# Down stage of a fused attention and gated-MLP block: the first outer Strassen product gets a second Strassen level

## The chip, the cores and the metric

The kernel runs on one core of one Trainium2 chip. The metric is the device time of one execution in microseconds; the matrix unit is TensorE (PE in the profile), the elementwise engines are VectorE (DVE), ScalarE (ACT) and GpSimd (POOL), and SyncE (SP) issues most of the DMA transfers. Each engine works through its own queue of instructions in order, and engines wait for one another by semaphores.

## The reference

The computation is one transformer block on 2048 tokens of width 1024 in bf16: a layer norm, linear attention with 32 heads, a residual, a second layer norm, a gated MLP of width 3584, and a residual.

```python
x = A_x
h = x + attention(layernorm(x), A_wqkv, A_wo)
n = layernorm(h)
gate, up = n @ B_W_gate, n @ B_W_up          # [2048, 1024] @ [1024, 3584]
hidden = (gate * (gate > 0)) * up
h2 = h + hidden @ B_W_down                   # [2048, 3584] @ [3584, 1024]
```

The change is in the last line's product, the down stage, and at its border with the gate/up stage before it.

## The kernel before

Most products are computed by Winograd's form of Strassen's algorithm: left and right operands are cut in two by two blocks, four sums of left blocks (s1 to s4) and four of right blocks (t1 to t4) are formed, and seven block products (m1 to m7) take the place of eight. With left blocks a11, a12, a21, a22 and right blocks b11 to b22:

- s1 = a21 + a22, s2 = s1 - a11, s3 = a11 - a21, s4 = a12 - s2
- t1 = b12 - b11, t2 = b22 - t1, t3 = b22 - b12, t4 = b21 - t2
- m1 = a11 b11, m2 = a12 b21, m3 = s4 b22, m4 = a22 t4, m5 = s1 t1, m6 = s2 t2, m7 = s3 t3

The partial sums of the products are formed in PSUM: m1, then m6, then m7, then m4 are accumulated in one and the same PSUM tile (tag A), and a copy or an add takes the running sum out after each of them. m2 has a tile of its own. m5 and then m3 accumulate in another one.

**Gate/up stage.** The hidden width is handled in 14 pairs of chunks of 128. One call of `quad` (L902) does the seven products for one chunk and one set of 512 tokens; a call is one window of the schedule, six products of eight 128x512 matmuls, while m4 and m3 of the previous window run inside it. ScalarE copies running sums (L921) and applies the ReLU (L926, L933). VectorE adds (L925), multiplies gate and up (L929, L936) and forms the sums of hidden blocks that the down stage will read (L751 to L759). These sums are stored to DRAM (L754, L761). The tiles of the block h11, which the first outer product reads, stay in SBUF as `x1`. In the first window of each later group of four, a further product over part of the contraction is itself done by Strassen (`cross`, L988); its operand sums and results live in tiles of a small pool: `cs` (left sums), `ct` (weight sums), and `cr` (results, read by `g0` of later windows). Each window has six slots (`slot`, L1071) in which pending VectorE work is put between the named steps. In the last two windows no such work is left.

**Down stage.** The outer level cuts tokens (two halves of 1024), hidden width (two halves of 14 chunks) and output columns (two halves of 512) and makes seven outer products, in the order 1, 2, 6, 5, 3, 7, 4 (`OUTER`, L1025). I call them op0 to op6. The left sums come from DRAM (`x_dram`), the weight sums too (`t_dram`).

- For the outer products in `INNER` (L1026) a second Strassen level is used (`inner`, L1387): seven products of 28 matmuls of 128x256, with 4 token tiles times 7 chunks. Its operand sums are formed by VectorE from a queue (`queue_sums`, L1306; `pop` takes the next one), and results leave by `snap` (L1415) and `sink` (L1422).
- op0 (outer product 1) and op5 (outer product 7) are plain (`plain_mm`, L1233): four pairs of token tiles times two contraction halves, each a block of 14 matmuls of 128x512.
- op0's result is copied by ScalarE to the fp32 tiles `u2` (`sink1`, L1470), four copies. Later products add to `u2` and `u5`.
- Outputs are put into the four-deep tile `o` by VectorE and stored by an accumulating DMA from GpSimd, or for the last product by a plain one (`put`, L1366). The residual h is loaded in `load_h` (L1359).

**Order.** TensorE, VectorE and ScalarE run in the order in which the program text issues their work from the start of the gate/up stage, and SP from the opening of `dpool` (L1266). Around the border the text is: m7 of the last window, op0's first plain block, then the last window's `g3`, `x3`, m4, `rg`, `x2`, m3, `g1`, `x1`. Then the gate/up pools are closed and `dpool` takes their memory. Then come the loads for op1 (L1463 to L1467), the other seven blocks of op0, and the loop over op1 to op6 (L1494). Within that loop a second-level product takes m4 and m3 of the second-level product before it in between its own m2 and m6.

Of the kernel before, what the change touches and what calls it, by code (L numbers as in the profile page):

```python
# [8 lines left out]
ALU = mybir.AluOpType  # L9
FP32 = mybir.dt.float32  # L10
# [72 lines left out]
def block_kernel(ctx: ExitStack, tc: tile.TileContext, x, wqkv, wo, wg, wu, wd, out, H: int):  # L83
# [195 lines left out]
    with ExitStack() as actx:  # L279
# [668 lines left out]
    KQ = KH // 2  # L948
    cross_s = [ipool.tile([P, KQ, SW], FP16, tag=f"cs{k}", name=f"cs{k}") for k in range(3)]
    cross_a = [[hnT[s][0][:, KH + j * KQ:KH + (j + 1) * KQ, :] for j in range(2)] for s in range(NS)]  # L950

    def cross_left_sums():

        (a11, a12), (a21, a22) = cross_a
        s1, s2, s4 = (v[:] for v in cross_s)
        tt = nc.vector.tensor_tensor
        return [
            lambda: tt(out=s1, in0=a21, in1=a22, op=ALU.add),
            lambda: tt(out=s2, in0=s1, in1=a11, op=ALU.subtract),
            lambda: tt(out=s4, in0=a12, in1=s2, op=ALU.subtract),  # L960
            lambda: tt(out=a21.bitcast(FP16), in0=a11, in1=a21, op=ALU.subtract),
        ]

    def cross_left(m):
        (a11, a12), (a21, a22) = cross_a
        s1, s2, s4 = (v[:] for v in cross_s)
# [120 lines left out]
    for r, (wt, f, fi, toks) in enumerate(runs):  # L1087
# [3 lines left out]
        for n, s in enumerate(toks):  # L1091
# [14 lines left out]
            if k:  # L1106
                want = -(-len(fill) // max(nwin - 2 - k, 1))
                for p in range(want):
                    work.insert(len(work) if held_back else min(len(work), 2 * p + 1), fill.pop(0))
            held_back = []  # L1110
            if k == NE and not snaps:
                base = [new_snap() for i in range(4)]
                res = {(0, 0): base[0], (1, 0): base[0]}
                for q in ((0, 1), (1, 1)):
                    res[q] = ipool.tile([P, 2, SW], FP32, tag=f"cr{q[0]}", name="cr")
                snaps.extend((base[1], base[3], base[2]))
                snaps.insert(0, snaps.pop())
# [123 lines left out]
    for i in range(NS):  # L1241
        for kh in range(2):
            xtiles[0, i, kh] = x1[i][kh][:]
    fview = []
    for n in range(2):
        t = fpool.tile([P, 4 * D], BF16, tag="wraw", bufs=2, name="xd")
        fview.append(t[:, 0:FQ * SW].rearrange("p (f t) -> p f t", f=FQ))
    ftile = fpool.tile([P, FQ * SW], BF16, tag="wt", name="xd")
    xs_free = [ftile[:, 0:FQ * SW].rearrange("p (f t) -> p f t", f=FQ).bitcast(FP16)]
    for i, t in ((1, fview[0]), (0, fview[1])):  # L1250
        xtiles[1, i, 0] = t
        load_x(1, i, 0)
    first_ps = [acc("A")]
    plain_mm(first_ps[0], 0, 0, 0)
    prv["g3"]()
    prv["x3"]()
    prv["m4"]()
    prv["rg"]()
    prv["x2"]()
    prv["m3"]()  # L1260
    prv["g1"]()
    prv["x1"]()
    sctx.close()
    mctx.close()

    dpool = ctx.enter_context(tc.tile_pool(name="dpool", **reuse))  # L1266
    ctx.enter_context(tc.manual_schedule(engines={ET.SP}))

    for x in range(2):
        wtiles[2 + x] = dpool.tile([P, FQ, DW], BF16, tag=f"w{x}", name="w")[:]  # L1270
        xtiles[1, 1 - x, 1] = dpool.tile([P, FQ, SW], BF16, tag=f"x{x}", name="x")[:]
    for x in range(3):
        xs_free.append(dpool.tile([P, FQ, SW], FP16, tag=f"xs{x}", name="xs")[:])
    held_s = {}
    free_s = list(range(4))

# [29 lines left out]
    def queue_sums(op):  # L1306
# [42 lines left out]

        queue.extend((op, f.__name__, f) for f in (t1, s1, s2, t2, s4, s3, t3, t4))  # L1350

    def new_u(nm):
        return [dpool.tile([P, NT, DW], FP32, tag=nm, bufs=2, name=nm) for s in range(NS)]

    u2, u5 = new_u("u2"), new_u("u5")
    out_v = of.rearrange("(t p) d -> p t d", p=P)
    hres = {}

    def load_h(k, s):  # L1359

        if k == OUTER[-1]:
            v = dpool.tile([P, NT, DW], BF16, tag="h", bufs=2, name="h")
            nc.scalar.dma_start(out=v[:], in_=h_dram[s][:])
            hres[k, s] = v

    def put(k, s, ts, cs, ps, m, with_h=True, eng=nc.scalar):  # L1366

        i, j = outs[k]
        o = dpool.tile([P, NT * HW], BF16, tag="o", bufs=4, name="o")
        ov = o[:, 0:(ts.stop - ts.start) * (cs.stop - cs.start)].rearrange("p (t d) -> p t d", t=ts.stop - ts.start)  # L1370
# [12 lines left out]

    base_of = {2: u2, 6: u2, 5: u2, 3: u5, 4: u2}
    u_of = {6: u2, 5: u5}

    def inner(op):  # L1387

        k, st, base = op["k"], {}, base_of[op["k"]]
        tag = "XY"[op["n"] % 2]  # L1390

# [29 lines left out]

        def sink(s, j, nm, m, ts=ALL, with_h=True):  # L1422
            m = base[s][:, ts, cols(j)] if m is None else st[m][:, ts]
            if k in u_of:
                add(out=u_of[k][s][:, ts, cols(j)], in0=view(nm)[:, ts], in1=m, op=ALU.add)
            else:
                put(k, s, ts, cols(j), view(nm)[:, ts], m, with_h)

        def tail_mm(m, start):
            need(op, *{3: ("s4",), 5: ("s1", "t1")}[m])  # L1430
            for h in range(2):
                if start:
                    st["E", h] = acc("XY"[(op["n"] + h) % 2])
                for tt in range(2):
# [35 lines left out]
    def sink1(p, ps):  # L1470
        s, t0 = divmod(2 * p, NT)
        nc.scalar.copy(out=u2[s][:, t0:t0 + 2, :], in_=ps[:].rearrange("p (t d) -> p t d", t=2))

    pss = first_ps + [acc(t) for t in ("A", "X", "Y")]
    for p in range(1, 4):
        plain_mm(pss[p], 0, p, 0)
    load_x(2, 0, 0)
    load_w(2, 0)
    load_x(2, 1, 0)
    pop(2)  # L1480
    for p in range(4):
        plain_mm(pss[p], 0, p, 1)
        sink1(p, pss[p])
        if p == 0:
            load_h(OUTER[1], 0)
            load_h(OUTER[1], 1)
        pop(2)
    load_x(2, 1, 1)
    load_w(2, 1)
    load_x(2, 0, 1)  # L1490
    queue_sums(ops[2])

    prv = None
    for n in range(1, len(OUTER)):  # L1494
# [4 lines left out]
        def early_loads():  # L1499
            if nxt and n > 1:  # L1500
                load_w(n + 1, 0)
                load_x(n + 1, 1, 0)

        def late_x():
            if nxt and n > 1:
                load_x(n + 1, 1, 1)

        def late_w():
            if nxt and n > 1:
                load_w(n + 1, 1)  # L1510
                if nxt["k"] in INNER:
                    queue_sums(nxt)
# [8 lines left out]
        if op["k"] in INNER:  # L1521
# [28 lines left out]
            if tail:  # L1550
                cur["h01"]()
                add(out=u2[1][:], in0=u2[1][:], in1=hres[op["k"], 1][:], op=ALU.add)
            pop(2)
# [14 lines left out]
        else:  # L1568
            pss = []
            for p in range(4):  # L1570
                ps = acc(("A", "A", "XY"[(n + 1) % 2], "XY"[n % 2])[p])
                plain_mm(ps, n, p, 0)
# [67 lines left out]
```

## Time and profile before

| What | Value |
| --- | --- |
| Median of 4 runs | 728.3 us (728.28 to 728.42) |
| Profiled execution, its own time | 728.28 us |
| Its span in the profile | 726.5 us |
| TensorE busy | 717.9 us, 99% of the span |
| VectorE busy | 583.0 us, 80% |
| ScalarE busy | 325.2 us, 45% |
| Plain blocks, op0 and op5 (L1237) | 224 matmuls of 128x512 |
| VectorE, 563.82 to 591.45 us (op0 and the end of the last window) | 12.98 of 27.63 us busy |
| VectorE, 591.45 to 606.73 us (op1's first five products) | 13.78 of 15.28 us busy |
| Data moved, 579.36 to 591.45 us | 402 GB/s |
| Data moved, 591.45 to 606.73 us | 398 GB/s |

A timeline line gives the start in microseconds from the start of the span, the length, the engine, the line of the program, the operation, the tile written and the tiles read, the shape, and the number of instructions merged into the line. A bracket gives the idle time of that engine before the line and what ended it. Matmuls overlap, so the length of a merged TensorE line is a little more than the distance to the next one. "SPq" lines are the issue of a DMA transfer, not the transfer.

### The profile page before, as it was taken

The page shows a single profiled execution, that of the slowest core. Times are in us where ns is not written, and L with a number is a line of the kernel's source. Part 1 is how long each engine was busy: PE and PEld are TensorE (multiplying, and loading weights), DVE is VectorE, ACT ScalarE, POOL GpSimd, SP SyncE. Part 2 cuts the span into 40 slices and gives each one's busy share as a digit, 9 for nine tenths or more (in the row PEclk, how much of TensorE's full clock was granted, in tenths as well). Part 3 has the DMA queues.
Part 4 walks back from the last instruction along what each step waited for, and adds up shares of the span by engine and source line. Part 5 has one row for each costly group of instructions (what it writes and reads, how often), then busy time and mean ns, then how long its engine had stood idle before and what let it go on. Part 6 is the DMA issues. An engine that isn't in the chain of part 4 may idle for free.

```text
span 726.5 us, 10634 instructions
## 1 busy us (share of the span) xinstructions
PE 717.9 (99%) x4000; PEld 379.4 (52%) x4000; DVE 583.0 (80%) x1039; ACT 325.2 (45%) x580; POOL 20.8 (3%) x56
## 2 busy tenths in 40 slices
PE   7999999999999999999999999999999999999997
PEld 3454555444444444444444444444444468888666
DVE  6998754777898776889998998988977379996677
ACT  4785653878886564344444454443444120000000
POOL 1000000000000000000000000000000001100210
PEclk9999999999999999999999999999999999999999
DMA  9666003089986523196556585565653499977932
GB/s 317 171 136 174 0 1 115 3 181 240 225 170 171 131 79 111 46 279 187 197 184 196 200 261 198 179 189 185 210 166 121 154 396 311 325 265 258 261 44 59
DMA packets 144708, 128.89 MB, mean 177 GB/s; under 512 B 50960, under 2 KB 127888, under 8 KB 144656
## 3 DMA queue, kind: packets, MB, share of 16 engines
q1 hardware_dynamic: 137584, 123.30, 56.0%
q0 software_dynamic: 5312, 3.15, 3.6%
q10 hardware_dynamic: 1760, 1.77, 0.7%
q8 instruction: 31, 0.51, 0.3%
q14 instruction: 21, 0.17, 0.1%
HBM read 76.81 MB, written 39.85 MB: 161 GB/s over the span
## 4 chain that ended last, share of the span: by engine, by line
PE 92%; DVE 4%; ACT 2%; DMA 1%; issue 0%; SPq 0%; DVEq 0%; ACTq 0%
PE accA L916 21%; PE accA L1411 8%; PE attn L608 7%; PE Aq L365 6%; PE accX L916 6%; PE accY L916 5%; PE accA L1237 3%; PE Aq L789 3%; PE Aq L505 3%; PE accX L1411 3%; PE Eq L365 3%; PE accY L1411 3%; PE accA L1004 2%; PE vp L416 2%; PE kp L398 2%; PE Eq L789 2%
## 5 line engine op out<-in xcount | busy, mean ns | idle before, releaser
L921 ACT COPY snap<-accA 128x1024 f32<-128x1024 f32 x52 | 52.4, 1010 | 66.1 <-PE accA L916 66.0
L926 ACT ACTIVATE gu<-gu 128x512 bf16<-128x512 bf16 x72 | 45.4, 630 | 79.3 <-DVE gu L925 79.2
L916 PEld LDWEIGHTS <-tg 128*128 128x128 f16 x384 | 37.4, 98 | 45.7 <-DVE tg L697 0.5
L916 PEld LDWEIGHTS <-tu 128*128 128x128 f16 x384 | 37.5, 98 | 45.4
L608 PE MATMUL attn<-wo_mem,oT 128*128 128x512 bf16 x256 | 59.0, 379 | 0.5 <-DVE o_sb L585 0.4
L916 PE MATMUL accA<-hn,tg 128*128 128x512 f16 (+1 forms) x192 | 49.3, 379 | 0.0
L916 PE MATMUL accA<-hn,tu 128*128 128x512 f16 (+1 forms) x192 | 49.3, 379 | 0.0
L205 ACT COPY u<-Aq 128x512 f32<-128x512 f32 x54 | 31.4, 581 | 36.5 <-PE Aq L365 19.7
L1411 PEld LDWEIGHTS <-x 128*128 128x128 f16 (+1 forms) x448 | 43.7, 98 | 5.6
L608 PEld LDWEIGHTS <-oT 128*128 128x128 bf16 x256 | 24.6, 97 | 29.9 <-issue 2.2
L925 DVE TENSOR_TENSOR gu<-accX,snap 128x1024 bf16<-128x1024 f32 x26 | 31.7, 1220 | 10.1 <-ACT snap L921 7.8
L925 DVE TENSOR_TENSOR gu<-accY,snap 128x1024 bf16<-128x1024 f32 x26 | 31.7, 1220 | 7.4 <-ACT snap L921 7.4
L916 PEld LDWEIGHTS <-wg 128*128 128x128 bf16 x208 | 20.3, 98 | 25.0 <-issue 0.5
L916 PEld LDWEIGHTS <-wu 128*128 128x128 bf16 x208 | 20.3, 98 | 24.6
L365 PEld LDWEIGHTS <-xT 128*128 128x128 bf16 (+1 forms) x192 | 18.6, 98 | 21.9 <-issue 0.3
L611 DVE SCALAR_TENSOR_TENSOR x_res<-attn,x_res 128x512 bf16<-128x512 f32 x32 | 22.0, 687 | 9.5 <-PE attn L608 9.3
L1375 POOL DMA_DIRECT2D out_dram<-o x12 | 15.2, 1265 | 502.0 <-DMA h<-h_dram 412.4
L585 DVE TENSOR_TENSOR o_sb<-nd,rd 128x384 bf16<-128x384 f32 (+1 forms) x48 | 23.7, 510 | 7.1 <-ACT rd L584 5.5
L1411 PEld LDWEIGHTS <-xs 128*128 128x128 f16 x280 | 27.4, 98 | 3.2
L1417 DVE TENSOR_TENSOR snap<-accA,u 128x1024 f32<-128x1024 f32 x16 | 19.5, 1221 | 11.4 <-PE accA L1411 11.3
L929 DVE TENSOR_TENSOR hq<-gu 128x512 bf16<-128x512 bf16 x48 | 20.3, 422 | 9.9 <-ACT gu L926 9.7
L1237 PEld LDWEIGHTS <-x 128*128 128x128 bf16 (+1 forms) x168 | 16.4, 98 | 19.6
(268 smaller groups left out, 1515.2 us busy)
## 6 DMA issues: line engine op xcount, KB each, us to landing
x<-x_dram SPq DMA_DIRECT2D x17, 896.0 KB, 9.0
x_dram<-hq SPq DMA_DIRECT2D x28, 512.0 KB, 3.0
wg<-in_B_W_gate_dram SPq DMA_DIRECT2D x14, 512.0 KB, 4.8
wu<-in_B_W_up_dram SPq DMA_DIRECT2D x14, 512.0 KB, 5.6
x_dram<-hq SPq DMA_DIRECT2D x28, 256.0 KB, 2.4
wraw<-in_B_W_down_dram SPq DMA_DIRECT2D x14, 512.0 KB, 4.3
t_dram<-wt SPq DMA_DIRECT2D x21, 256.0 KB, 2.2
xd<-x_dram SPq DMA_DIRECT2D x6, 896.0 KB, 6.7
```

The costliest lines, as they stand in the source:

```text
L205: copies[nm, v] = nc.scalar.copy(out=snaps[nm, v], in_=bank[v][:])
L365: nc.tensor.matmul(ps[:], lhsT=left[m - 1][:, kc, r + v * P:r + (v + 1) * P], rhs=right[m - 1][:, kc, :], start=(start and kc == 0), stop= ...
L585: nc.vector.tensor_tensor(out=ov[:, c0:c0 + n], in0=ndv[:, :, 0:P].rearrange("p k (h e) -> p k h e", h=HPC), in1=rd[:, 0:n, :].unsqueeze(3 ...
L608: nc.tensor.matmul(ps[:], lhsT=st["oT"][:, c, :], rhs=wo_sb[:, c, j * NW:(j + 1) * NW], start=(c == 0), stop=(c == KC - 1))
L611: added[t, j] = nc.vector.scalar_tensor_tensor(out=h_sb[:, j * NW:(j + 1) * NW], in0=ps[:], scalar=1.0, in1=h_sb[:, j * NW:(j + 1) * NW], ...
L789: nc.tensor.matmul(ps[:], lhsT=w(v, m)[:, kc, :], rhs=left[m - 1][:, kc, :], start=(start and kc == 0), stop=(kc == KH - 1), skip_group_ch ...
L916: nc.tensor.matmul(ps[:, v, :], lhsT=w[v][n - 1][:, kc, :], rhs=left[n - 1][:, kc, :], start=(t is not None and kc == 0), stop=(kc == KH - ...
L921: nc.scalar.copy(out=st[nm][:], in_=halves(st["A"]))
L925: add(out=g[:], in0=halves(st[nm]), in1=st[base][:], op=ALU.add)
L926: nc.scalar.activation(out=g[:, 0, :], in_=g[:, 0, :], func=ACT.Relu)
L1237: nc.tensor.matmul(ps[:, t * NW:(t + 1) * NW], lhsT=x_tile(n, s, kh)[:, f, (t0 + t) * P:(t0 + t + 1) * P], rhs=w_tile(n, kh)[:, f, :], sta ...
L1411: nc.tensor.matmul(pv[:, tt, :], lhsT=left(m)[:, f, tt * P:(tt + 1) * P], rhs=right(m)[:, f, :], start=(t is not None and f == 0 and tt % ...
```

## The change

op0 becomes a second-level product like op1 to op4 and op6: 196 matmuls of 128x256 instead of 112 of 128x512.

- Its operand sums are formed in other places than those of later products. t1 goes into `ct`, t2 into `cs`, s1 into `cr`, s2 into the fp16 view of the `wt` tile, s4 into the first of the `xs` tiles. t3 and t4 overwrite halves of the weight tiles and s3 overwrites `x1[1][0]`.
- t1, t2 and t3 are put into the second last window's slots 3 to 5, s1 and s2 (six of seven chunks) into slots 3 and 4 of the last window. s3 (six chunks) follows `x3` at the border, and the seventh chunk of s1, s2 and s3 follows `x1`. t4 and s4 are issued after the add "00".
- `cs`, `cr` and `ct` are kept for the whole kernel, in a pool that is not closed; `cs` and `cr` become one tile each. The output buffers `o` are now four pieces of `ct` and `cs`, and h is loaded into `cr`.
- op0's results go to `u2` by four ScalarE copies (after m1, m6, m7, m4) and three VectorE adds ("00", "11", "01").
- op0's m4 and m3 now run inside op1, as between later products. op1's loads come in another order, op2's loads move into the loop, and op1's sums are queued with t2 second.
- The PSUM tags X and Y continue the alternation of the windows (`tagof`).

```diff
-    ipool = sctx.enter_context(tc.tile_pool(name="ipool", side="right", **reuse))
+    ipool = ctx.enter_context(tc.tile_pool(name="ipool", side="right", **reuse))
...
-    cross_s = [ipool.tile([P, KQ, SW], FP16, tag=f"cs{k}", name=f"cs{k}") for k in range(3)]
+    cross_sb = ipool.tile([P, 3, KQ, SW], FP16, tag="cs", name="cs")
+    cross_s = [cross_sb[:, k] for k in range(3)]
...
+    cross_r = ipool.tile([P, NS, 2, SW], FP32, tag="cr", name="cr")
...
-    INNER = (2, 6, 5, 3, 4)
+    INNER = (1, 2, 6, 5, 3, 4)
...
+    first_s, first_t, xs_free = {}, {}, []
+
+    def first_weight_sums():
+
+        tt = nc.vector.tensor_tensor
+        first_t["t1"] = cross_t[:].rearrange("p a b c d -> p (a b c d)")[:, 0:FQ * HW].rearrange("p (f d) -> p f d", f=FQ)
+        first_t["t2"] = cross_sb[:].rearrange("p a b c -> p (a b c)")[:, 0:FQ * HW].rearrange("p (f d) -> p f d", f=FQ)
+
+        def b(i, j):
+            return wtiles[i][:, :, j * HW:(j + 1) * HW]
+
+        def t3():
+            first_t["t3"] = b(0, 1).bitcast(FP16)
+            tt(out=first_t["t3"], in0=b(1, 1), in1=b(0, 1), op=ALU.subtract)
+
+        def t4():
+            first_t["t4"] = b(1, 0).bitcast(FP16)
+            tt(out=first_t["t4"], in0=b(1, 0), in1=first_t["t2"], op=ALU.subtract)
+
+        return [
+            lambda: tt(out=first_t["t1"], in0=b(0, 1), in1=b(0, 0), op=ALU.subtract),
+            lambda: tt(out=first_t["t2"], in0=b(1, 1), in1=first_t["t1"], op=ALU.subtract),
+            t3, t4,
+        ]
+
+    def first_left_sums(f):
+
+        tt = nc.vector.tensor_tensor
+
+        def a(i, j):
+            return x1[i][j][:, f, :]
+
+        def s1():
+            if "s1" not in first_s:
+                v = cross_r[:].rearrange("p a b c -> p (a b c)").bitcast(FP16)
+                first_s["s1"] = v[:, 0:FQ * SW].rearrange("p (f t) -> p f t", f=FQ)
+            tt(out=first_s["s1"][:, f, :], in0=a(1, 0), in1=a(1, 1), op=ALU.add)
+
+        def s2():
+            if "s2" not in first_s:
+                t = fpool.tile([P, FQ * SW], BF16, tag="wt", name="xd")
+                xs_free.append(t[:, 0:FQ * SW].rearrange("p (f t) -> p f t", f=FQ).bitcast(FP16))
+                first_s["s2"] = xs_free[0]
+            tt(out=first_s["s2"][:, f, :], in0=first_s["s1"][:, f, :], in1=a(0, 0), op=ALU.subtract)
+
+        def s3():
+            first_s["s3"] = x1[1][0][:].bitcast(FP16)
+            tt(out=a(1, 0).bitcast(FP16), in0=a(0, 0), in1=a(1, 0), op=ALU.subtract)
+
+        def s4():
+            first_s["s4"] = xs_free[1]
+            tt(out=xs_free[1][:, f, :], in0=a(0, 1), in1=first_s["s2"][:, f, :], op=ALU.subtract)
+
+        return [s1, s2, s3, s4]
+
+    first_w = first_weight_sums()
+    bulk = first_left_sums(slice(0, FQ - 1))
+    last = first_left_sums(slice(FQ - 1, FQ))
...
+            if k >= nwin - 2:
+                work += [lambda: None] * 3 + (first_w[:3] if k == nwin - 2 else bulk[:2])
...
-        queue.extend((op, f.__name__, f) for f in (t1, s1, s2, t2, s4, s3, t3, t4))
+        queue.extend((op, f.__name__, f) for f in ((t1, t2, s1, s2, s4, s3, t3, t4) if op["n"] == 1 else (t1, s1, s2, t2, s4, s3, t3, t4)))
...
+    o_free = [v[:, i * NT * HW:(i + 1) * NT * HW].bitcast(BF16)
+              for v in (cross_t[:].rearrange("p a b c d -> p (a b c d)"), cross_sb[:].rearrange("p a b c -> p (a b c)"))
+              for i in range(2)]
...
-            v = dpool.tile([P, NT, DW], BF16, tag="h", bufs=2, name="h")
+            v = cross_r[:, s].rearrange("p a b -> p (a b)").bitcast(BF16).rearrange("p (t d) -> p t d", t=NT)
...
-        o = dpool.tile([P, NT * HW], BF16, tag="o", bufs=4, name="o")
+        o_free.append(o_free.pop(0))
...
         def snap(nm, s, j):
+            if base is None:
+                nc.scalar.copy(out=u2[s][:, :, cols(j)], in_=view("A"))
+                return
...
         def sink(s, j, nm, m, ts=ALL, with_h=True):
+            if base is None:
+                v = u2[s][:, :, cols(j)]
+                if m is None:
+                    nc.scalar.copy(out=v, in_=view(nm))
+                else:
+                    add(out=v, in0=view(nm), in1=v, op=ALU.add)
+                return
...
-    first_ps = [acc("A")]
-    plain_mm(first_ps[0], 0, 0, 0)
+    ops[0].update(s=first_s, t=first_t)
+    cur = inner(ops[0])
+    cur["m1"]()
     prv["g3"]()
     prv["x3"]()
+    bulk[2]()
     prv["m4"]()
     prv["rg"]()
     prv["x2"]()
     prv["m3"]()
     prv["g1"]()
     prv["x1"]()
+    for f in last[:3]:
+        f()
     sctx.close()
     mctx.close()
...
     load_w(1, 0)
+    load_w(1, 1)
+    load_x(1, 0, 1)
     load_x(1, 1, 1, slice(0, FQ - 1))
-    load_w(1, 1)
     load_x(1, 1, 1, slice(FQ - 1, FQ))
-    load_x(1, 0, 1)
     queue_sums(ops[1])
+    cur["s1"]()
+    cur["m2"]()
+    cur["00"]()
+    first_w[3]()
+    first_left_sums(slice(0, FQ))[3]()
+    cur["m6"]()
+    cur["m5"]()
+    cur["s2"]()
+    pop(2)
+    cur["m7"]()
     load_x(2, 0, 0)
-    load_w(2, 0)
-    load_x(2, 1, 0)
...
     load_x(2, 0, 1)
-    queue_sums(ops[2])
-
-    prv = None
+    cur["s3"]()
+
+    prv = cur
```

The diff leaves out the removed plain blocks and `sink1` of op0, the PSUM tags, and the conditions in the loop that had exempted op1.

More of the change, by code (lines that the diff above doesn't have):

```diff
@@ L954, in cross_left_sums @@
         (a11, a12), (a21, a22) = cross_a
-        s1, s2, s4 = (v[:] for v in cross_s)
+        s1, s2, s4 = cross_s
         tt = nc.vector.tensor_tensor
@@ L965, in cross_left @@
         (a11, a12), (a21, a22) = cross_a
-        s1, s2, s4 = (v[:] for v in cross_s)
+        s1, s2, s4 = cross_s
         return (a11, a12, s4, a22, s1, s2, a21.bitcast(FP16))[m - 1]
+    cross_r = ipool.tile([P, NS, 2, SW], FP32, tag="cr", name="cr")
     cross_t = ipool.tile([P, 2, 4, KQ, P], FP16, tag="ct", name="ct")
@@ L1114, in block_kernel @@
                 for q in ((0, 1), (1, 1)):
-                    res[q] = ipool.tile([P, 2, SW], FP32, tag=f"cr{q[0]}", name="cr")
+                    res[q] = cross_r[:, q[0]]
                 snaps.extend((base[1], base[3], base[2]))
@@ L1243, in block_kernel @@
             xtiles[0, i, kh] = x1[i][kh][:]
[L1244 to L1252, printed above, removed]
-    first_ps = [acc("A")]
-    plain_mm(first_ps[0], 0, 0, 0)
[L1255 to L1275, printed above, removed]
+    held_s = {"s1": 3, "s2": 0, "s4": 1}
+    free_s = [2]
     def new_op(n):
@@ L1348, in s4 @@
             tt(out=new_s("s4"), in0=a(0, 1), in1=S["s2"], op=ALU.subtract)
-        queue.extend((op, f.__name__, f) for f in (t1, s1, s2, t2, s4, s3, t3, t4))
-    def new_u(nm):
-        return [dpool.tile([P, NT, DW], FP32, tag=nm, bufs=2, name=nm) for s in range(NS)]
-    u2, u5 = new_u("u2"), new_u("u5")
+        queue.extend((op, f.__name__, f) for f in ((t1, t2, s1, s2, s4, s3, t3, t4) if op["n"] == 1 else (t1, s1, s2, t2, s4, s3, t3, t4)))
     out_v = of.rearrange("(t p) d -> p t d", p=P)
     hres = {}
+    o_free = [v[:, i * NT * HW:(i + 1) * NT * HW].bitcast(BF16)
+              for v in (cross_t[:].rearrange("p a b c d -> p (a b c d)"), cross_sb[:].rearrange("p a b c -> p (a b c)"))
+              for i in range(2)]
     def load_h(k, s):
         if k == OUTER[-1]:
-            v = dpool.tile([P, NT, DW], BF16, tag="h", bufs=2, name="h")
-            nc.scalar.dma_start(out=v[:], in_=h_dram[s][:])
+            v = cross_r[:, s].rearrange("p a b -> p (a b)").bitcast(BF16).rearrange("p (t d) -> p t d", t=NT)
+            nc.scalar.dma_start(out=v, in_=h_dram[s][:])
             hres[k, s] = v
@@ L1368, in put @@
         i, j = outs[k]
-        o = dpool.tile([P, NT * HW], BF16, tag="o", bufs=4, name="o")
-        ov = o[:, 0:(ts.stop - ts.start) * (cs.stop - cs.start)].rearrange("p (t d) -> p t d", t=ts.stop - ts.start)
+        o_free.append(o_free.pop(0))
+        ov = o_free[-1][:, 0:(ts.stop - ts.start) * (cs.stop - cs.start)].rearrange("p (t d) -> p t d", t=ts.stop - ts.start)
         add(out=ov, in0=ps, in1=m, op=ALU.add)
@@ L1382, in cols @@
         return slice(j * HW, (j + 1) * HW)
-    base_of = {2: u2, 6: u2, 5: u2, 3: u5, 4: u2}
-    u_of = {6: u2, 5: u5}
+    base_of, u_of = {}, {}
+    tagof = [new_tag() for n in range(len(OUTER))]
     def inner(op):
-        k, st, base = op["k"], {}, base_of[op["k"]]
-        tag = "XY"[op["n"] % 2]
+        k, st, base = op["k"], {}, base_of.get(op["k"])
+        tag = tagof[op["n"]]
         def left(m):
@@ L1432, in tail_mm @@
                 if start:
-                    st["E", h] = acc("XY"[(op["n"] + h) % 2])
+                    st["E", h] = acc(tagof[op["n"] - h])
                 for tt in range(2):
@@ L1460, in inner @@
         }
-    ops = [new_op(n) for n in range(len(OUTER))]
+    fview = []
+    for n in range(2):
+        t = fpool.tile([P, 4 * D], BF16, tag="wraw", bufs=2, name="xd")
+        fview.append(t[:, 0:FQ * SW].rearrange("p (f t) -> p f t", f=FQ))
+    for i, t in ((1, fview[0]), (0, fview[1])):
+        xtiles[1, i, 0] = t
+        load_x(1, i, 0)
+    ops = [new_op(n) for n in range(len(OUTER))]
+    ops[0].update(s=first_s, t=first_t)
+    cur = inner(ops[0])
+    cur["m1"]()
+    prv["g3"]()
@@ new lines, in block_kernel @@
+    prv["x3"]()
+    bulk[2]()
+    prv["m4"]()
+    prv["rg"]()
+    prv["x2"]()
+    prv["m3"]()
+    prv["g1"]()
+    prv["x1"]()
+    for f in last[:3]:
+        f()
+    sctx.close()
+    mctx.close()
+    dpool = ctx.enter_context(tc.tile_pool(name="dpool", **reuse))
+    ctx.enter_context(tc.manual_schedule(engines={ET.SP}))
+    for x in range(2):
+        wtiles[2 + x] = dpool.tile([P, FQ, DW], BF16, tag=f"w{x}", name="w")[:]
+        xtiles[1, 1 - x, 1] = dpool.tile([P, FQ, SW], BF16, tag=f"x{x}", name="x")[:]
@@ L1463, in block_kernel, with new_u @@
+    for x in range(3):
+        xs_free.append(dpool.tile([P, FQ, SW], FP16, tag=f"xs{x}", name="xs")[:])
+    def new_u(nm):
+        return [dpool.tile([P, NT, DW], FP32, tag=nm, bufs=2, name=nm) for s in range(NS)]
+    u2, u5 = new_u("u2"), new_u("u5")
+    base_of.update({2: u2, 6: u2, 5: u2, 3: u5, 4: u2})
+    u_of.update({6: u2, 5: u5})
     load_w(1, 0)
+    load_w(1, 1)
+    load_x(1, 0, 1)
     load_x(1, 1, 1, slice(0, FQ - 1))
-    load_w(1, 1)
     load_x(1, 1, 1, slice(FQ - 1, FQ))
-    load_x(1, 0, 1)
@@ L1468, in block_kernel @@
     queue_sums(ops[1])
[L1470 to L1476, printed above, removed]
-    load_x(2, 0, 0)
-    load_w(2, 0)
-    load_x(2, 1, 0)
[L1480 to L1487, printed above, removed]
@@ L1488, in block_kernel @@
-    load_x(2, 1, 1)
-    load_w(2, 1)
+    cur["s1"]()
[8 more added lines that the diff above has]
+    cur["m7"]()
+    load_x(2, 0, 0)
     load_x(2, 0, 1)
-    queue_sums(ops[2])
-    prv = None
+    cur["s3"]()
+    prv = cur
     for n in range(1, len(OUTER)):
@@ L1499, in early_loads @@
         def early_loads():
-            if nxt and n > 1:
+            if nxt:
                 load_w(n + 1, 0)
@@ L1504, in late_x @@
         def late_x():
-            if nxt and n > 1:
+            if nxt:
                 load_x(n + 1, 1, 1)
         def late_w():
-            if nxt and n > 1:
+            if nxt:
                 load_w(n + 1, 1)
@@ L1551, in block_kernel @@
                 cur["h01"]()
-                add(out=u2[1][:], in0=u2[1][:], in1=hres[op["k"], 1][:], op=ALU.add)
+                add(out=u2[1][:], in0=u2[1][:], in1=hres[op["k"], 1], op=ALU.add)
             pop(2)
@@ L1570, in block_kernel @@
             for p in range(4):
-                ps = acc(("A", "A", "XY"[(n + 1) % 2], "XY"[n % 2])[p])
+                ps = acc(("A", "A", tagof[n - 1], tagof[n])[p])
                 plain_mm(ps, n, p, 0)
```

## The prediction

> **What bounds the kernel now.** I read the page's busy row and its chain first, then the TensorE timeline over the end of the gate/up stage and the first two outer products of the down stage, then VectorE, ScalarE and the SP queue over the same microseconds.
>
> ```profile
> PE 717.9 (99%) x4000; PEld 379.4 (52%) x4000; DVE 583.0 (80%) x1039; ACT 325.2 (45%) x580; POOL 20.8 (3%) x56
> ...
> PE 92%; DVE 4%; ACT 2%; DMA 1%; issue 0%; SPq 0%; DVEq 0%; ACTq 0%
> ```
>
> TensorE is busy for 99% of the span and makes 92% of the chain that ended last, so a matmul taken away is time taken away, as long as nothing makes TensorE wait. The place of the change (TensorE timeline: start, length, tiles, count):
>
> ```profile
> 563.82 3.19 PE L1237 MATMUL accA<-wd,x 128*128 128x512 bf16 x14
> 566.85 1.03 PE L916 MATMUL accA<-hn,tg 128*128 128x512 bf16 x4
> ...
> 568.57 1.03 PE L916 MATMUL accX<-hs,wg 128*128 128x512 f16 x4
> ...
> 570.30 3.19 PE L1237 MATMUL accA<-wd,x 128*128 128x512 bf16 x14
> 573.32 3.18 PE L1237 MATMUL accX<-wd,x 128*128 128x512 bf16 x14
> ...
> 588.43 3.19 PE L1237 MATMUL accY<-wd,x 128*128 128x512 bf16 x14
> 591.45 3.22 PE L1411 MATMUL accA<-w,xd 128*128 128x256 bf16 x28
> 594.51 3.22 PE L1411 MATMUL accY<-w,x 128*128 128x256 bf16 x28
> ```
>
> No row has an idle bracket: TensorE runs without a gap. Lengths overlap, so I count from start to start: a plain block of 14 takes 573.32 - 570.30 = 3.02 us (216 ns a matmul), a second-level product of 28 takes 594.51 - 591.45 = 3.06 us (109 ns a matmul). What else is running there (VectorE, ScalarE, SP):
>
> ```profile
> 565.07 1.23 DVE L925 TENSOR_TENSOR gu<-accX,snap 128x1024 bf16<-128x1024 f32 x1 [2.04 <-ACT snap L921]
> ...
> 569.46 0.69 DVE L936 TENSOR_TENSOR hq<-accA,rg 128x512 bf16<-128x512 f32 x1 [2.05 <-ACT rg L933]
> ...
> 571.32 1.22 DVE L925 TENSOR_TENSOR gu<-accX,snap 128x1024 bf16<-128x1024 f32 x1
> 573.30 0.42 DVE L929 TENSOR_TENSOR hq<-gu 128x512 bf16<-128x512 bf16 x1 [0.76 <-ACT gu L926]
> ...
> 580.14 1.09 DVE L1325 TENSOR_TENSOR ws<-w 128x1792 f16<-128x1792 bf16 x1 [5.96 <-DMA w<-in_B_W_down_dram]
> 585.04 2.02 DVE L1338 TENSOR_TENSOR xd<-xd,x 128x3584 f16<-128x3584 bf16 x1 [3.81 <-DMA x<-x_dram]
> ...
> 572.63 0.63 ACT L926 ACTIVATE gu<-gu 128x512 bf16<-128x512 bf16 x1 [3.21 <-DVE gu L925]
> ...
> 574.66 0.42 SPq L1042 DMA_DIRECT2D w<-in_B_W_down_dram  x1
> ```
>
> VectorE has holes of about 2 us in the last two gate/up windows and a long one afterwards, ended by loads for the second outer product (called op1; the changed one is op0). SP cannot issue those loads before 574.66.
>
> **Removed.** op0's eight plain blocks: 8 x 3.02 = 24.18 us. **Added on TensorE.** Seven products of 28: 7 x 3.06 = 21.40 us. Net -2.78 us. The Trainium skill (TensorE: Matmul & The Clock Gate, Back-to-back issue gap) speaks against halving the columns: it gives a sustained stream of weight loads and matmuls about 131 ns a matmul at 512 columns and 81 ns at 128, so the weight load weighs more when columns are few. An estimate halfway, 98 ns at 256, makes 112 x 131 = 14.7 us into 196 x 98 = 19.2 us, a loss of 4.5 us. This kernel's own rows say 216 and 109 ns, and its weight loads take 98 ns, inside the 109; the rows decide.
>
> **Added on VectorE.** Four weight sums of 1792 columns (1.08 us each, row at 580.14) and four left sums of 3584 (2.02 each, row at 585.04), three of the latter cut into 3072 + 512 columns (about 1.75 from those two rows, and 0.42 from the 512-column row). In the built order t1, t2 and t3 follow the `g1` add and `x1` of the second last window. They fill its 0.76 and 2.04 us holes and move the next `g3` from 554.71 to about 554.75: free. In the last window s1 (3072) stands before `x1`, s2 after it. `x1` goes from 562.14 to 563.0; s2 runs 563.8 to 565.6; the `g3` add moves from 565.07 to 565.5 and ends at 566.7. Its reader on TensorE, the m3 that reuses that bank, starts at 568.6, so this is covered by 1.9 us. With `x3` at 567.4, s3 (3072) runs from 567.75 to 569.5, where VectorE was idle until 569.46 (`x2`). So `x2` and everything after it is late by 0.04 us only. Cover gone, each of these would cost its overrun.
>
> **The new wait.** op0 now accumulates m1, m6, m7 and m4 in one PSUM bank, with a ScalarE copy after each, and m6 may not start before the copy of m1 is out. That copy stands on ScalarE behind the last ReLU of the gate/up stage (row at 572.63), which waits for the `g1` add (571.32), which is queued behind `x2` and its three sums. Worked through with the +0.04: ReLU at 572.67, the copy 0.53 later (step between ScalarE rows at 557.16 and 557.69), 1.01 long (the 128x1024 copies), and 0.05 to TensorE (a VectorE add ending at 329.60 released a matmul at 329.65): m6 at 574.26. TensorE would be there at 563.82 + 3.06 + 3.45 (last m4, m3) + 3.06 (m2) = 573.39. Wait: 0.87 us. Second part: the weights of m6's seventh matmul are the last row of s2, two short sums behind `x1` and L759 on VectorE: 573.33, 573.79, 574.13, 574.59, ending at 575.01; with 0.05 and a 0.10 weight load that is 575.16, against 574.26 + 6 x 0.109 = 574.92. With 0.04 for rounding, another 0.28. Total 1.15 us. Queued behind the waiting m6 are m5, m7 and all of op1, so TensorE pays it fully. The clock should not move: its granted mean is 1.00 in each stretch from 100 to 700 us, and the same page (What's actually happening) wants some 3.4 us of idleness before it throttles; no run here shows a gap of this kind. If it did throttle, half speed over a window of 3.4 us would add 1.7 us.
>
> **The other sinks.** Four ScalarE copies stay four (1.01 each). Three VectorE adds of 1.22 us come on top ("00", "11", "01"). "00" at 575.3 is done a microsecond before m5 at 577.6 reuses its bank; "11" at 585 lies 8 us before m3 needs the bank; "01" follows m3. None ends a TensorE wait.
>
> **Moved: op1's loads and sums.** op1's m1 now starts at 583.7, not 591.45. The queue's order becomes both weight halves, x(0,1), then x(1,1) in two parts. SP still issues the first at 574.7 (behind the last x_dram store) and it lands at 580.2: 3.5 us to spare. In the old order 2.75 MB had landed by 585.04; the new order puts 0.92 MB more ahead of x(1,1), and the stage moves 400 GB/s, so it lands at about 587.3 and the other two by 585 (m2 wants them at 586.8). VectorE's s1 of op1 waits for it and holds the queue: op1's snapshot, "00", s2 (593.7; m6 wants it at 595.9), s4, "01", s3, snapshot, t3 (601.4; m7 wants it at 602.1). The landing may slip a microsecond before TensorE waits. SP next stands still for op2's first x, whose buffers s3 (575.4) and s4 (579.6) still read; behind it queue only loads for op2, whose own buffers come free at 583.7 and later. h's load moves behind op0's last copy (about 594) and meets op2's loads, whose last is due at 608 and lands by 605. In op2 to op4 the same reckoning has t3 done about 0.6 us before m7 starts, since m4 and m3 of the product before now come in between. The 12 outgoing stores use old buffers with the same four-deep turn: nothing.
>
> **Sum.** -2.78 + 1.15 = -1.63 us; op2 starts at 605.1 instead of 606.73, and after it the TensorE order is the old one. The profiled execution took 728.28 us (726.5 span and 1.8 around it), the median of the runs shown is 728.3: 726.65 us. The wait's ends: 0.87 if the seventh matmul's weights are in time, 1.7 if VectorE runs half a microsecond later than reckoned: 726.4 to 727.2.
>
> **Rivals.** (a) The wait is hidden and all 2.78 us arrive: 725.5. For it: TensorE is the bound and every sum lies in holes. Against it: ScalarE is in order and m6 needs the copy. (b) Part of the gain is lost again in op1 to op4, because x(1,1) lands at 589 or t3 misses its 0.6 us: each loses 0.5 to 1 us, 727.2 to 728.5. For it: DMA is busy without a break in this stage (9s in the page). Against it: the old run shows no TensorE wait there. (c) Slower: VectorE becomes the bound of op1 to op4. t3 ends 0.6 us ahead of m7; if VectorE runs later than that, every product waits for it anew. To lose 1.63 + 1.46 us over four places t3 has to be 1.4 us later than reckoned: then 729.8, and 731 with 1.7 us. Against it: VectorE's rows there still have waits on TensorE in them. (d) Built otherwise than said: no, the built order has 196 matmuls of 256 columns for op0.
>
> **How the numbers follow.** 0.2% (1.46 us) is about what a measurement of this kernel can tell from no change: faster means under 726.84. Main case 0.70, own range 726.3 to 727.2, and four fifths of it under 726.84; (a) 0.07; (b) 0.16, all of it within 0.2% either way; (c) 0.07. Faster 0.56 + 0.07 = 0.63, same 0.14 + 0.16 = 0.30, slower 0.07. The range takes in (a) and most of (b): 725.4 to 728.2.
>
> **What would show it.** In the new timeline: op0's products 3.06 us apart; one TensorE idle of 0.7 to 1 us at about 573.4, released by the ScalarE copy, a smaller one released by the short sum; op2's m1 at about 605.1. A TensorE wait after 590 means (b) or (c); no idle at 573.4 means (a). Wrong would be the sum if a VectorE sum of 3072 columns took longer than 1.75 us, or x(1,1) landed after 588.3.

## The result and the profile after

The changed kernel takes 727.16 us (median), the kernel before 728.43 us over the runs beside it: ratio 0.9983, 95% interval 0.9978 to 0.9988, so 1.27 us by the medians. The profiled execution took 726.77 us with a span of 725.0 us. In it op2's m1 starts 605.24 - 563.90 = 41.34 us after op0's m1; before, it was 606.73 - 563.82 = 42.91 us. From op0 to op1 this execution gained 1.57 us, and from op2's m1 on the order is the old one. The row of op2's m1 before:

```profile
606.73 3.22 PE L1411 MATMUL accA<-wd,x 128*128 128x256 f16 x28
```

The page after, the busy row and the chain:

```profile
PE 715.5 (99%) x4084; PEld 387.5 (53%) x4084; DVE 597.6 (82%) x1053; ACT 325.0 (45%) x580; POOL 20.8 (3%) x56
...
PE 91%; DVE 4%; ACT 2%; DMA 1%; issue 0%; SPq 0%; DVEq 0%; ACTq 0%
```

TensorE has 84 more matmuls and is busy 2.4 us less; VectorE is busy 14.6 us more. TensorE's timeline after, over op0, op1 and the start of op2 (start, length, tiles, count, idle time before and its releaser):

```profile
563.90 3.22 PE L1442 MATMUL accA<-wd,x 128*128 128x256 bf16 x28
566.96 1.03 PE L916 MATMUL accA<-hn,tg 128*128 128x512 bf16 x4
...
570.41 3.22 PE L1442 MATMUL accY<-wd,x 128*128 128x256 bf16 x28
574.33 3.39 PE L1442 MATMUL accA<-cs,xd 128*128 128x256 f16 x28 [0.70 <-ACT u L1448]
577.56 3.22 PE L1442 MATMUL accY<-ct,cr 128*128 128x256 f16 x28
580.62 3.22 PE L1442 MATMUL accA<-wd,x 128*128 128x256 f16 x28
583.68 3.22 PE L1442 MATMUL accA<-w,xd 128*128 128x256 bf16 x28
586.73 3.22 PE L1442 MATMUL accX<-w,x 128*128 128x256 bf16 x28
...
598.96 3.22 PE L1442 MATMUL accX<-ws,xs 128*128 128x256 f16 x28
602.19 3.22 PE L1442 MATMUL accA<-w,xd 128*128 128x256 f16 x28
605.24 3.22 PE L1442 MATMUL accA<-wd,x 128*128 128x256 f16 x28
```

A product takes 3.06 us from start to start when nothing stops it. Measured so, m2 to m6 is 3.92 us: m6 waits 0.86 us. (The bracket says 0.70, because it counts from the modelled end of the matmul before, which overlaps.) m6 itself takes 3.23 us, 0.17 too long: its seventh weight load (PEld in the profile) waits for the last row of s2. And op1's m5 at 598.96 is followed by m7 only at 602.19, 0.17 us late and without a bracket. The three waits make 1.20 us. The seventh weight load:

```profile
575.15 0.88 PEld L1442 LDWEIGHTS <-xd 128*128 128x128 f16 x9 [0.28 <-DVE xd L1098]
```

In what follows x(0,1) and x(1,1) are the two blocks of op1's left operand that are loaded from DRAM behind the border (`load_x(1, 0, 1)` and, in two parts, `load_x(1, 1, 1)`). VectorE in the same execution:

```profile
563.87 1.75 DVE L1098 TENSOR_TENSOR xd<-cr,x 128x3072 f16<-128x3072 f16 x1
565.53 1.22 DVE L925 TENSOR_TENSOR gu<-accX,snap 128x1024 bf16<-128x1024 f32 x1
...
569.58 0.69 DVE L936 TENSOR_TENSOR hq<-accA,rg 128x512 bf16<-128x512 f32 x1
...
574.67 0.42 DVE L1098 TENSOR_TENSOR xd<-cr,x 128x512 f16<-128x512 f16 x1
...
584.01 1.09 DVE L1360 TENSOR_TENSOR ws<-w,ws 128x1792 f16<-128x1792 bf16 x1 [2.85 <-DMA w<-in_B_W_down_dram]
...
588.46 2.02 DVE L1370 TENSOR_TENSOR xs<-xd,x 128x3584 f16<-128x3584 bf16 x1 [2.23 <-DMA x<-x_dram]
...
601.06 1.08 DVE L1364 TENSOR_TENSOR w<-w 128x1792 f16<-128x1792 bf16 x1
```

The last row is t3 of op1: it ends at 602.14, and m7 starts 0.05 later. What put it there is the row at 588.46, s1 of op1, which stood 2.23 us for x(1,1); from then on VectorE works without a gap of more than 0.1 us. And ScalarE, around the copy of m1:

```profile
572.75 0.63 ACT L926 ACTIVATE gu<-gu 128x512 bf16<-128x512 bf16 x1 [3.21 <-DVE gu L925]
573.29 1.00 ACT L1448 COPY u<-accA 128x1024 f32<-128x1024 f32 x1
```

The copy had its input from 567.12 on, when m1 ended, and stood behind the ReLU.

### The profile page after: what moved, and what is told of

It is laid out like the page before. It is cut to its first block, busy times and chain, and to the rows that moved or that the text cites. A ratio compares the mean times of both kernels' runs of the same rounds, so it can differ in the third digit from the quotient of the medians.

```text
span 725.0 us, 10812 instructions
## 1 busy us (share of the span) xinstructions
PE 715.5 (99%) x4084; PEld 387.5 (53%) x4084; DVE 597.6 (82%) x1053; ACT 325.0 (45%) x580; POOL 20.8 (3%) x56
## 4 chain that ended last, share of the span: by engine, by line
PE 91%; DVE 4%; ACT 2%; DMA 1%; issue 0%; SPq 0%; DVEq 0%; ACTq 0%
PE accA L916 21%; PE accA L1442 10%; PE attn L608 7%; PE Aq L365 6%; PE accY L916 6%; PE accX L916 5%; PE accY L1442 4%; PE Aq L789 3%; PE Aq L505 3%; PE Eq L365 3%; PE accX L1442 3%; PE accA L1006 2%; PE vp L416 2%; PE kp L398 2%; PE Eq L789 2%; PE accA L1299 2%
## 5 line engine op out<-in xcount | busy, mean ns | idle before, releaser
L1442 PEld LDWEIGHTS <-x 128*128 128x128 f16 (+1 forms) x560 | 54.7, 98 | 7.3
L608 PEld LDWEIGHTS <-oT 128*128 128x128 bf16 x256 | 24.6, 98 | 29.8 <-issue 2.1
L916 PEld LDWEIGHTS <-wu 128*128 128x128 bf16 x208 | 20.3, 98 | 24.6
L1442 PEld LDWEIGHTS <-xd 128*128 128x128 f16 (+1 forms) x280 | 27.3, 98 | 4.5 <-issue 1.1
L1442 PE MATMUL accA<-wd,x 128*128 128x256 f16 (+1 forms) x252 | 29.0, 273 | 0.0
L1442 PEld LDWEIGHTS <-xs 128*128 128x128 f16 x252 | 24.6, 98 | 2.9
L916 PE MATMUL accA<-hs,tg 128*128 128x512 f16 x96 | 24.7, 380 | 0.0
```

What stands on the lines that cost most here:

```text
L608: nc.tensor.matmul(ps[:], lhsT=st["oT"][:, c, :], rhs=wo_sb[:, c, j * NW:(j + 1) * NW], start=(c == 0), stop=(c == KC - 1))
L916: nc.tensor.matmul(ps[:, v, :], lhsT=w[v][n - 1][:, kc, :], rhs=left[n - 1][:, kc, :], start=(t is not None and kc == 0), stop=(kc == KH - ...
L1442: nc.tensor.matmul(pv[:, tt, :], lhsT=left(m)[:, f, tt * P:(tt + 1) * P], rhs=right(m)[:, f, :], start=(t is not None and f == 0 and tt % ...
```

## The experiments

Two theories stood against each other: only the wait at m6 costs, so that taking it away brings the rest of the 2.78 us; or op1's loads are a second limit just behind it, and what is won in op0 is waited for in op1. To keep early differences between executions out, I give the distance from op0's m1 to op2's m1 in each profile beside the median. The ratio has the late executions in it (up to 729.49 us for the changed kernel), which the median hardly feels, so the two do not always agree.

| Kernel | op0's m1 to op2's m1, us | Median, us | Ratio to before (95%) |
| --- | --- | --- | --- |
| before | 42.91 | 728.43 | |
| changed | 41.34 | 727.16 | 0.9983 (0.9978 to 0.9988) |
| changed, again | 41.38 | 727.18 | 0.9982 (0.9975 to 0.9989) |
| copy early | 41.45 | 727.31 | 0.9986 (0.9978 to 0.9995) |
| rows whole | 41.74 | 727.26 | 0.9984 (0.9977 to 0.9990) |
| both: no m6 wait | 41.67 | 727.21 | 0.9983 (0.9975 to 0.9990) |
| t3 early | 41.28 | 726.75 | 0.9982 (0.9975 to 0.9988) |
| no m6 wait, t3 early | 41.11 | 726.50 | 0.9975 (0.9967 to 0.9982) |
| old order of loads | 43.01 | 728.56 | 1.0001 (0.9993 to 1.0009) |
| early weights | 41.17 | 726.63 | 0.9973 (0.9964 to 0.9983) |
| all, early weights | 40.13 | 725.64 | 0.9966 (0.9952 to 0.9979) |
| all, once more | 40.14 | 725.69 | 0.9966 (0.9953 to 0.9978) |

**The changed kernel again.**

> The changed kernel once more, beside the others on one chip. Theory (two waits): TensorE loses 1.15 us at op0's m6 and 0.2 to 0.6 us at op1's m7, which waits for t3 behind the late x(1,1); time about 1.2 us under the kernel before. Rival (only the m6 wait counts): 1.6 us under.

The median repeats. In this profile op1's m7 starts 603.33 - 600.05 - 3.06 = 0.22 us late.

**The copy of m1 early.**

```diff
-                nc.scalar.copy(out=u2[s][:, :, cols(j)], in_=view("A"))
+                if nm == "m1":
+                    st["c"] = cross_sb[:].rearrange("p a b c -> p (a b c)")[:, FQ * HW:FQ * HW + NT * HW]
+                    nc.scalar.copy(out=st["c"], in_=st["A"][:])
+                else:
+                    nc.scalar.copy(out=u2[s][:, :, cols(j)], in_=view("A"))
...
     prv["rg"]()
+    cur["s1"]()
     prv["x2"]()
...
     queue_sums(ops[1])
-    cur["s1"]()
     cur["m2"]()
```

> The changed kernel with only the copy of m1 ahead of the last ReLU, into a free piece of cs; the last rows of s1, s2 and s3 stay where they are. If the m6 wait has two releasers in series, m6 starts on time (about 573.5) and stops at its seventh matmul until about 575.2: no gain, op1's m1 at about 583.7. If the copy alone makes the wait: 0.9 us gained in op0.

TensorE's timeline of this kernel:

```profile
573.45 0.82 PE L1442 MATMUL accA<-cs,xd 128*128 128x256 f16 x6
575.13 2.58 PE L1442 MATMUL accA<-cs,xd 128*128 128x256 f16 x22 [0.86 <-DVE xd L1098]
577.54 3.22 PE L1442 MATMUL accY<-ct,cr 128*128 128x256 f16 x28
```

m6 starts on time, does six matmuls and stops for the last row of s2. m5 starts at 577.54, as in the changed kernel. The two releasers are in series, and taking the first away brings nothing. (The add "00" reads the new place. The new place is an fp16 tile: this kernel, and the three below that hold the same edit, keep m1 in half precision for that add, where the changed kernel keeps it in fp32. ScalarE's copy takes 1.01 us all the same.)

**s1, s2 and s3 whole.**

```diff
-    bulk = first_left_sums(slice(0, FQ - 1))
-    last = first_left_sums(slice(FQ - 1, FQ))
+    bulk = first_left_sums(slice(0, FQ))
...
-    bulk[2]()
     prv["m4"]()
...
-    for f in last[:3]:
-        f()
...
     cur["00"]()
+    bulk[2]()
     first_w[3]()
```

> The changed kernel with s1 and s2 formed whole in the last window and s3 whole after the add 00; the copy of m1 stays behind the last ReLU. If the two releasers are in series, m6 still waits 0.86 us for the copy, and its seventh matmul no longer waits: op0's wait falls from 1.03 to 0.86 us. If the loads bound op1, those 0.17 us come back as a longer wait at op1's m7, and the time is that of the changed kernel, 727.2 us.

TensorE's timeline:

```profile
574.24 3.22 PE L1441 MATMUL accA<-cs,xd 128*128 128x256 f16 x28 [0.70 <-ACT u L1447]
...
602.49 3.22 PE L1441 MATMUL accA<-w,xd 128*128 128x256 f16 x28 [0.57 <-DVE w L1363]
```

m5 starts at 577.29, 6.97 us after m2 (570.32): 6.11 us is two products, so op0's wait is 0.86. op1's m7 now waits 602.49 - 598.71 - 3.06 = 0.72 us. More came back than the 0.17 us that was won; x(1,1) landed at 588.76 here.

**Both: no wait at m6.** The two edits above together.

> op0's m6 has nothing to wait for: the copy of m1 goes to a free piece of the cs tile ahead of the last ReLU, s1 and s2 are formed whole in the last window, s3 whole after the add 00. Theory (two waits): m6 starts on time at about 573.5, but x(1,1) lands at the same 588.5, so VectorE's t3 for op1 is done at the same 602.1 and op1's m7 waits about 1.3 us instead of 0.2; no gain over the changed kernel within 0.2 us, op2's m1 at about 605.2. Rival (only the m6 wait counts): 1.15 us faster than the changed kernel, op2's m1 at about 604.1.

TensorE's timeline:

```profile
573.47 3.22 PE L1441 MATMUL accA<-cs,xd 128*128 128x256 f16 x28
...
582.64 3.22 PE L1441 MATMUL accA<-w,xd 128*128 128x256 bf16 x28
586.48 3.23 PE L1441 MATMUL accX<-w,x 128*128 128x256 bf16 x28 [0.62 <-DMA x<-x_dram]
...
598.72 3.22 PE L1441 MATMUL accX<-ws,xs 128*128 128x256 f16 x28
602.51 3.22 PE L1441 MATMUL accA<-w,xd 128*128 128x256 f16 x28 [0.57 <-DVE w L1363]
```

op0 runs without a gap and op1's m1 starts a microsecond earlier, at 582.64. Then m2 waits 0.78 us for x(0,1), and m7 waits 0.73 us for t3. All of it is given back: op1's waits make 1.51 us here against 0.17 in the changed kernel, for the 1.03 us won in op0. The theory with a second limit holds; that part of the wait falls on m2 was not in its expectation. In the changed kernel x(0,1) had landed at about 586.1 (10.1 us after its issue at 576.01), only 0.6 us before m2 started.

**t3 and t4 of op1 early**, in the changed kernel.

```diff
-        queue.extend((op, f.__name__, f) for f in ((t1, t2, s1, s2, s4, s3, t3, t4) if op["n"] == 1 else (t1, s1, s2, t2, s4, s3, t3, t4)))
+        queue.extend((op, f.__name__, f) for f in ((t1, t2, t3, t4, s1, s2, s4, s3) if op["n"] == 1 else (t1, s1, s2, t2, s4, s3, t3, t4)))
...
     cur["s2"]()
-    pop(2)
+    pop(4)
     cur["m7"]()
...
-            pop(2)
+            pop(0 if n == 1 else 2)
             cur["m7"]()
```

> The changed kernel with op1's t3 and t4 formed right after t2, in the hole in which VectorE waits for x(1,1). Theory (two waits): op1's m7 starts without a wait, op2's m1 0.17 us earlier in the profile; the median 0.3 to 0.5 us under the changed kernel's, and the spread of the runs narrower. Rival (only the m6 wait counts): no difference in time or spread.

VectorE's timeline:

```profile
584.14 1.08 DVE L1364 TENSOR_TENSOR w<-w 128x1792 f16<-128x1792 bf16 x1
...
589.13 2.02 DVE L1370 TENSOR_TENSOR xs<-xd,x 128x3584 f16<-128x3584 bf16 x1 [1.76 <-DMA x<-x_dram]
```

t3 lies in the hole, x(1,1) lands even later (589.13), and m7 (602.12) starts 3.06 us after m5 (599.06) all the same. In this profile only 0.06 of the expected 0.17 us arrives, because m2 now starts 586.83 - 583.66 - 3.06 = 0.11 us late, behind x(0,1). The median is 0.41 us lower, as expected, and 14 of the 21 runs lie under 726.9 us, against 11 of 54 of the changed kernel. The ratio with its interval does not tell the two apart. The spread is narrower only in its lower half (0.20 us against 0.53). That the runs of the changed kernel wait 0.4 to 0.5 us at m7, where the profiles show 0.17 and 0.22, is inferred from this median and the one with early weights; no profile shows such a run.

**No m6 wait and t3 early.**

> Both edits together. Theory (two waits): m6 without a wait, op1's m7 limited by s4, the add 01, s3 and the snapshot behind x(1,1), about 601.2: some 1.0 us faster than the changed kernel, 2.2 us under the kernel before. It is up to 0.7 us less if op1's m2, now due at 585.6, waits for x(0,1). Rival (only the m6 wait counts): the same time as the kernel without the m6 wait.

TensorE's timeline:

```profile
583.28 3.22 PE L1441 MATMUL accA<-w,xd 128*128 128x256 bf16 x28
587.30 3.23 PE L1441 MATMUL accX<-w,x 128*128 128x256 bf16 x28 [0.80 <-DMA x<-x_dram]
```

This execution is 0.64 us late from before op0 on. m7 starts without a wait, but m2 now waits 587.30 - 583.28 - 3.06 = 0.96 us for x(0,1). With VectorE out of the way the loads hold TensorE directly; of the microsecond expected, 0.23 us arrives in this profile and 0.66 in the median. The expectation had named this wait as what could take up to 0.7 us of it.

**The old order of op1's loads**, in the changed kernel.

```diff
     load_w(1, 0)
-    load_w(1, 1)
-    load_x(1, 0, 1)
     load_x(1, 1, 1, slice(0, FQ - 1))
+    load_w(1, 1)
     load_x(1, 1, 1, slice(FQ - 1, FQ))
+    load_x(1, 0, 1)
```

> The changed kernel with op1's loads in the order of the kernel before: w(0), x(1,1) but its last row, w(1), the last row, x(0,1). If the loads bound op1, x(0,1) lands last at about 588.5, op1's m2, due at 586.7, waits about 1.7 us, and the time is 1.3 to 1.6 us over the changed kernel, no faster than the kernel before. If loads are hidden: no change.

TensorE's timeline:

```profile
583.72 3.22 PE L1442 MATMUL accA<-w,xd 128*128 128x256 bf16 x28
588.61 3.23 PE L1442 MATMUL accX<-w,x 128*128 128x256 bf16 x28 [1.67 <-DMA x<-x_dram]
```

m2 is 1.83 us late, m7 on time, and the gain is gone. op1's two weight halves and two x blocks share one queue and have all landed only at about 588.5, as in the changed kernel; the order chooses who waits.

**Early weights**, in the changed kernel. op1's weight halves go into the tiles `hn` of the token set that is finished, so that they can be loaded two windows earlier; three of the four snapshot tiles go into `hs` to make room.

```diff
-        aops = mctx.enter_context(tc.tile_pool(name=f"aops{s}", reuse_waits="tile", bufs=1))
+        aops = (mctx if s else ctx).enter_context(tc.tile_pool(name=f"aops{s}", reuse_waits="tile", bufs=1))
...
+            if k == nwin:
+                for x in range(2):
+                    wtiles[2 + x] = hnT[0][x][:].rearrange("p a b -> p (a b)")[:, 0:FQ * DW].rearrange("p (f d) -> p f d", f=FQ)
+                    load_w(1, x)
...
+    snap_free = [v[:].rearrange("p a b -> p (a b)").bitcast(FP32).rearrange("p (t d) -> p t d", t=NT) for v in hns[0]]
...
-    load_w(1, 0)
-    load_w(1, 1)
     load_x(1, 0, 1)
```

The cut leaves out the new turn of the snapshot tiles and the two weight tiles that are no longer taken from `dpool`.

> The changed kernel with only the early weight loads. If the loads bound op1, x(1,1) lands near 584 and op1 has no wait; the m6 wait stays: op2's m1 41.2 us after op0's m1, about 726.7 us. If not: 727.2 us.

The issue of the weights, m5 and m7 of op1:

```profile
545.11 0.38 SPq L1044 DMA_DIRECT2D hn<-in_B_W_down_dram  x1
556.98 0.37 SPq L1044 DMA_DIRECT2D hn<-in_B_W_down_dram  x1
...
598.96 3.22 PE L1447 MATMUL accX<-ws,xs 128*128 128x256 f16 x28
602.02 3.22 PE L1447 MATMUL accA<-hn,xd 128*128 128x256 f16 x28
```

op0's wait stays, op1 has none, and both numbers are met.

**All of it: no m6 wait, t3 early, early weights.**

> No m6 wait and t3 early, and in addition op1's two weight halves are loaded during the last windows into the operand tiles hn of the finished token set, so that only x(0,1) and x(1,1) are loaded after 574.8. If the loads bound op1: no TensorE wait is left in op0 and op1, op2's m1 comes 40.1 us after op0's m1 (41.3 in the changed kernel, 42.9 before), 725.6 us: the whole 2.78 us. If not: the time of the run with both waits out, 726.5 us.

TensorE's timeline:

```profile
573.54 3.22 PE L1446 MATMUL accA<-cs,xd 128*128 128x256 f16 x28
...
585.77 3.22 PE L1446 MATMUL accX<-hn,x 128*128 128x256 bf16 x28
...
601.05 3.22 PE L1446 MATMUL accA<-hn,xd 128*128 128x256 f16 x28
604.11 3.22 PE L1446 MATMUL accA<-wd,x 128*128 128x256 f16 x28
```

No idle bracket is left. 42.91 - 40.13 = 2.78 us, the whole of what the matmul count promised, and 725.64 us in the median.

> The kernel with early weight loads, t3 early and no m6 wait once more, for a narrower interval: 725.6 us, 2.8 us under the kernel before.

It repeats at 725.69 us and 40.14 us. Each time four of five runs lie between 725.5 and 725.8 and one at 727.6. This is the fastest kernel of the case: 2.8 us under the kernel before and 1.5 us under the changed one.

## Why the prediction was right, and where it was off

The forecast was 726.65 us, faster, in 725.4 to 728.2; measured was 727.16, inside the main case's own range and 0.5 us off the point. Of that half microsecond, 0.15 us lies in the kernel before, which ran at 728.43 beside the changed one and not at the 728.28 from which the sum started; 0.36 us lies in the gain, 1.63 us forecast and 1.27 us measured. The gain is 0.17%, just under the 0.2% by which I had divided faster from no change, so the outcome I gave 0.63 is not the one that came; the interval, 0.12% to 0.22%, contains the dividing line.

- The matmul count: -2.78 us forecast, 2.78 us in the kernel without waits. (The factors as printed, 8 x 3.02 and 7 x 3.06, make 24.16 and 21.42; 24.18 and 21.40 come from the unrounded distances between the rows.) The loss of 4.5 us, estimated between the two figures of the Trainium skill (TensorE: Matmul & The Clock Gate, Back-to-back issue gap), does not come: here the products take 109 ns a matmul, the plain blocks 216, and the measurement decides. (98 ns is a third of the way between the figures by columns, not half.)
- VectorE's sums in the holes: right to 0.1 us. s2 was placed at 563.8 to 565.6, `g3` at 565.5, `x2` late by 0.04; the trace has 563.87 to 565.62, 565.53, and `x2` at 569.58 with the whole execution 0.08 later. The sum of 3072 columns took 1.75 us, as reckoned.
- The new wait: right in mechanism. First part 0.87 forecast, 0.86 measured; second part 0.28 forecast, 0.17 measured. The forecast had put 0.10 for a weight load and 0.04 for rounding on top; the trace shows next to nothing of them, since the stopped load starts at 575.15, 0.06 after the short sum ends.
- The clock: no drop. The granted clock is 1.00 from 563.90 to 605.24, a product after the wait takes 3.06 us as before it, and the clock is 1.00 also around the longer gap of the old order of loads (1.67 us). The 1.7 us that the prediction would have added for a throttled window did not come.
- **The term that was mis-sized: op1's wait, set to zero.** The step said that x(1,1) lands at about 587.3 and may slip a microsecond before TensorE waits. It landed at 588.46, past the 588.3 that the prediction itself gave as a sign of being wrong, and t3 ended at 602.14 instead of 601.4. That is a wait of 0.17 us in the profile, and by the medians with t3 early and with early weights some 0.4 to 0.5 us in the ordinary run. Less the 0.12 us by which the m6 wait was smaller than forecast, this comes to about the missing 0.36.
- Why x(1,1) was late: the step took the old landing and added 0.92 MB at 400 GB/s. In the first 5.2 us the DMA engines moved 263 GB/s, against 293 in the old trace: 0.16 MB less, an estimated 0.4 us. And until the landing 4.75 MB had moved since the first load was issued, against 3.46 MB until 585.04 in the old trace: 1.29 MB more, not 0.92. The other 0.37 MB, an estimated 0.9 us at 400 GB/s, did not belong to op1's loads, which are 3.67 of the 4.75 MB. Two x loads of op2 were issued into the same queue at 577.9 and 579.56; the step placed them behind x(1,1) and counted no traffic of theirs before its landing. No run held them back, so that they are the cause is not shown.
- In the profile the sum of the waits came out almost as forecast, 1.20 us against 1.15. This is in part luck: 0.12 too much at m6 stands against 0.17 left out at op1's m7.
- Rival (a), all 2.78 us, falls: m6 does wait. Rival (b) named the right place, the late x(1,1), and by the prediction's own sign, a TensorE wait after 590, it came true beside the main case; its loss of 0.5 to 1 us was too large, and the waits stand in op1 alone. It ought to have been part of the main case with a share of its size, since a margin of one microsecond on an estimated landing is not a margin. Rival (c) falls: op2 to op4 show no TensorE wait.

What stays open, besides this, is how much the landing varies from run to run; only profiled executions show it. Counted from op0's m1, op1's s1 gets x(1,1) 24.6 us later in both profiles of the changed kernel, and 24.7 to 25.2 us later in the five other kernels that load the weights after 574.8 and x(1,1) last.

## What to carry to other kernels

When work is taken off the engine that bounds, everything it had been hiding comes nearer by the same amount: list the next two or three things that must be ready, with the margin of each, and count a margin smaller than the error of its estimate as a loss with a probability. Of two releasers of one instruction, taking away the first alone brought nothing here, and taking away both still brought nothing (727.21 us) while a late load stood behind them; so an edit that brings no time may still be half of a pair that does. A load that waits for a pool to close may have an older tile to go to: here two transfers moved some 18 and 30 us earlier, which was worth 0.5 us alone and 0.9 us, the last of the gain, once the other waits were out.

## What was not expected

The last three columns of these rows are the granted clock, the mean busy share of the DMA engines and the GB/s that they moved; the first row is of the kernel before, three are of the changed one, and the last is of the kernel with all edits and early weights:

```profile
574.80:580.00 5.20, 5.20 (x25) 2.35 (x24) 0.00 (x0) 0.00 (x0) 0.00 (x0) 1.00 0.94 293
...
574.80:580.00 5.20, 5.20 (x49) 4.42 (x47) 4.70 (x5) 1.01 (x1) 0.00 (x0) 1.00 0.87 263
580.00:584.00 4.00, 4.00 (x39) 3.57 (x37) 1.09 (x1) 0.12 (x1) 0.00 (x0) 1.00 1.04 384
584.00:588.50 4.50, 4.50 (x44) 4.02 (x42) 2.27 (x3) 0.89 (x1) 0.00 (x0) 1.00 1.03 414
...
574.80:580.00 5.20, 5.20 (x50) 4.66 (x49) 5.20 (x4) 1.01 (x1) 0.00 (x0) 1.00 0.92 317
```

With the weights first in the queue, its first five microseconds moved 263 GB/s at 0.87 of the DMA engines' time, and the 8.5 us after that 384 and 414 GB/s at full occupation. In the kernel with only x in the queue the same five microseconds moved 317 GB/s. What of this is the start of a queue and what is the form of the weight rows was not separated.
